# First batch of a fused attention and SiLU kernel: three score buffers instead of two, scores of four heads at once, two value passes in one PSUM bank, and half of w_in loaded in two quarters

## The chip, the cores and the metric

The kernel runs on one core of a Trainium2 chip. The metric is the device time of one execution in microseconds (us); the time before is a median of 391.56 us over three runs (391.54 to 392.47).

## The reference

Attention over 8 batches of 12 heads, 448 tokens and head size 64, and then a feed-forward layer with SiLU over the 3584 tokens:

```
scores = (q @ k^T) / sqrt(64)            # 8 x 12 x 448 x 448
attn   = exp(scores - max) / (sum + 1e-9)
x      = (attn @ v), heads side by side  # 3584 x 768
h      = x @ w_in                        # 3584 x 2048
out    = (h * sigmoid(h)) @ w_out        # 3584 x 768
```

All inputs and the output are float32; the kernel casts to f16 in its loads.

## The kernel before, in words

**Units.** The 12 heads are three groups of four. A unit is one batch and one head group. Batch 0 is cut in two pieces of 224 queries, so it has six units (0 to 5: units 0, 1, 2 are the first piece of the three groups, units 3, 4, 5 the second); `NB0` is 6. Every later batch has three units of 448 queries. A unit of batch 0 has two bursts of scores, the first over 256 keys, the second over 192.

**Attention of one unit.** TensorE writes the scores of a burst (line 346): each of the four heads of the group has its own 32 rows of the array, since head size 64 is split into two passes of 32. The destination is a pair of score tiles `s`, tile y for heads 2y and 2y+1, each of two PSUM banks (`score_banks`, line 336; two buffers, tag "s"). ScalarE turns each tile into `E` by one Exp of 896 elements a row (line 383). TensorE then makes three passes over `E` with four column strips of 32 (line 409): part 0 with a matrix of ones (the sums), parts 1 and 2 with the even and odd columns of `V`. Each part has a PSUM bank of its own (tag "m", four buffers). VectorE turns the sums (450), takes reciprocals (458), turns them back (464) and scales parts 1 and 2 into `xT` (480, one instruction each).

**Feed-forward.** `ffn1` (line 492 inside `times`) multiplies `xT` by `w_in`: for a piece of batch 0, 16 blocks of six matmuls of 224 columns, two blocks to a bank `h`. ScalarE takes the tanh (526), VectorE the gate (561). Then products with `w_out`: `o` for the first two row tiles (`plain`, in pieces of four blocks over 16; blocks 8 to 11 need the third quarter of `w_out`, 12 to 15 the fourth), `p` for the others.

**PSUM.** Eight banks: two `s` tiles of two banks and four `m` banks, for the whole run.

**Loads.** All loads go through GpSimd's DMA queue in one written order: k and q of the three groups of batch 0, V of batch 0 (four loads), q of units 3 and 4, the first half of `w_in` (three loads of 512 KB), q of unit 5, k and q of unit 6, the second half of `w_in`, k and q of unit 7, two quarters of `w_out`, k and q of unit 8, V of batch 1 (twelve loads), the other two quarters of `w_out`, and then batch by batch. Eight semaphores are used in turn, so a load is issued only when the one eight places before it has landed.

**Who sets the order.** A planner written in Python (`Order`, line 82, and the loop from line 1500 on) runs once while the program is built. It gives each operation a cost and a due time, keeps rings of buffers, and writes out the order of each engine's instructions; the engines then run these orders with semaphores. At line 1317 `split` makes the units below `HALVES` (5) issue the scores of heads 0, 1 and of heads 2, 3 as two separate operations; units from 5 on issue all four heads in one, tile y = 0 and y = 1 alternating inside. Matmuls on a tile of zeros (`run_zeros`, line 1491) fill waits of TensorE until the first `ffn1`.

Of the kernel before, what the change touches and what calls it, by code (L numbers as in the profile page):

```python
# [19 lines left out]
DMA_ROW = 0.022  # L20
DMA_RATE = 13570.0
DMA_START = 1.2
DMA_TAIL = 1.0
# [33 lines left out]

def when(deps):

    at = 0.0  # L60
    for d in deps:
        d, slack = d if isinstance(d, tuple) else (d, 0.0)
        if d is None or d.done is None:
            return None
        at = max(at, d.done - slack)
    return at
# [15 lines left out]
class Order:  # L82


    def __init__(self, shy):
        self.now, self.shy = 0.0, shy
        self.free = {"PE": 1.0, "ACT": 2.1, "DVE": 1.2, "POOL": 1.2}
        self.wait = {"ACT": [], "DVE": []}
        self.pool = []
        self.dma_free = 0.0  # L90
        self.out = []
        self.mode = None
        self.busy = {e: 0.0 for e in self.free}
# [8 lines left out]
    def start(self, op):  # L102
        self.emit(op.emit)
        self.free[op.eng] = self.now + op.busy
        self.busy[op.eng] += op.busy
        op.done = self.now + op.busy + op.tail
        if op.then:
            op.then(op.done)
# [12 lines left out]
    def step(self):  # L121
# [26 lines left out]
        elif self.pool:  # L148
            op, took, ring, gate = self.pool[0]
            at = 0.0  # L150
            if ring is not None:
                at = ring.when(1)
            if at is not None and gate is not None:
                g = gate()
                at = None if g is None else max(at, g)
            if at is not None and at <= self.now:
                self.pool.pop(0)
                if ring is not None:
                    ring.take()
                self.start(op)  # L160
                self.dma_free = max(self.dma_free, self.now + DMA_START) + took
                op.done = self.dma_free + DMA_TAIL
                soon.append(self.free["POOL"])
            elif at is not None:
                soon.append(at)
# [4 lines left out]
def kernel(  # L170
# [33 lines left out]
    HALVES = 5  # L204
    NEAR, LATE = 0.15, -2.0
# [14 lines left out]
    ps = ctx.enter_context(tc.tile_pool(name="ps", bufs=1, space=bass.MemoryType.PSUM))  # L220
    ctx.enter_context(
# [114 lines left out]
    def score_banks(n, w, ys):  # L336
        for y in ys:
            pS_t[(n, w, y)] = ps.tile(
                [128, 2, 512], FP32, name=f"s_{n}_{w}_{y}", tag="s", bufs=2
            )  # L340

# [75 lines left out]
    def attend_sums(ns):  # L417
        a = ps.tile([128, 512], FP32, name=f"a_{ns[0]}_0", tag="m", bufs=4)
# [14 lines left out]
    def attend(ns, part, n):  # L433
# [3 lines left out]
        acc[(n, part)] = ps.tile([128, 512], FP32, name=f"a_{n}_{part}", tag="m", bufs=4)  # L437
# [37 lines left out]
    def norm(n, part):  # L475
        b, hg, g0, g1 = units[n]
        nq = 32 * (g1 - g0)
        cc = 2 * hg + part - 1
# [24 lines left out]
    def ffn1(b, f, t0, t1, strips):  # L503
        i = f % blocks(b)
        if i == 0:
            h_t[(b, f, t0)] = ps.tile(
                [128, 512], FP32, name=f"h_{b}_{f}_{t0}", tag="m", bufs=4
            )
# [135 lines left out]
    def pair_product(f, m, strips):  # L644
        if m in (2, 5):
            t = ps.tile([128, 512], FP32, name=f"f_{f}_{m}", tag="m", bufs=4)
# [71 lines left out]
    def product(qd, m, strips):  # L718
        w = {1: rows(2 * qd, 0), 2: rows(2 * qd, 1), 4: rows(2 * qd + 1, 1), 7: rows(2 * qd + 1, 0)}
        w = w[m] if m in w else S_t[(qd, m)]  # L720
        if BANK[m] == m:
            pr_t[(qd, m)] = ps.tile([128, 512], FP32, name=f"p_{qd}_{m}", tag="m", bufs=4)
# [11 lines left out]
    def plain(t, j, f0, f1, strips):  # L734
        if f0 == 0:
            pr_t[("o", t, j)] = ps.tile([128, 512], FP32, name=f"o_{t}_{j}", tag="m", bufs=4)
# [27 lines left out]
    def store(qd, i, j):  # L764
        u, t = divmod(2 * qd + i, NT)
        w, turn = 0, 0
        while w < 4:
# [3 lines left out]
            if b == B - 1:  # L771
                n = 2
# [29 lines left out]
    s_ring, m_ring, e_ring = Ring(2), Ring(4), Ring(NE)  # L802
# [43 lines left out]
    plan_w_in(0, DFF // 2)  # L846
# [55 lines left out]

    moe = []
# [9 lines left out]
    def queue_ffn1(b, g0, g1):  # L913
        t0, t1, parts = 32 * g0, 32 * g1, []
        for f in range(NFF) if b == 0 else [x for f in range(HF) for x in (f, f + HF)]:

            def run(f=f):
                strips = b > 0 and od.mode == "cols" and bool(qk_seq or av_seq)
                op = Op("PE", NDC * mm(t1 - t0), lambda: ffn1(b, f, t0, t1, strips), tail=PE_OUT)
                if warm["on"]:  # L920
                    warm["on"] = False
                    m_ring.give(od.now)
                n = blocks(b)
                if f % n == 0:
                    m_ring.take()
                od.on_pe(op, "cols" if strips else "full")
                ffn1_left[b] -= 1
                if f % n < n - 1:
# [12 lines left out]
                    then=m_ring.give,  # L941
# [81 lines left out]
    def queue_pair_f(f):  # L1023
# [18 lines left out]
        def queue(m):  # L1042
# [6 lines left out]
            def run():  # L1049
                strips = od.mode == "cols" and bool(av_seq)  # L1050
                op = Op("PE", 3 * mm(S), lambda: pair_product(f, m, strips), tail=PE_OUT)
                if m in (2, 5):
                    m_ring.take()
# [10 lines left out]
                elif m == 2:  # L1064
                    read("11", "DVE", lambda: pair_add(f, "p", "B"), [op, done["p"]], m_ring.give)
# [4 lines left out]
                elif m == 3:  # L1070
                    read("12", "DVE", lambda: pair_add(f, "u", "C"), [op, done["u"]], m_ring.give)
# [26 lines left out]
    def sums_w(ms):  # L1098

        for m in ms:  # L1100
# [4 lines left out]
                        0.9,  # L1105
# [10 lines left out]
    def queue_plain(t, j):  # L1116
        parts = []

        def then(at):
            m_ring.give(at)  # L1120
            ost_ring.give(at + STORE)

        def queue(f0, f1):
            def run():
# [4 lines left out]
                if f0 == 0:  # L1129
                    m_ring.take()  # L1130
# [39 lines left out]
    def plan_sums():  # L1170
# [13 lines left out]
        while todo and (todo[0] == 7 or sg_ring.can(1, od.now)):  # L1184
# [4 lines left out]
            for f0 in (0, 4):  # L1189
                deps = [x for f in range(f0, f0 + 4) for x in gates[f] + gates[f + HF]]  # L1190
                if m != 5:
# [5 lines left out]
                            0.34,  # L1197
# [10 lines left out]
    def queue_quad(qd):  # L1208
# [4 lines left out]
        def read(m, deps):  # L1213
            def then(at):
                if m in (2, 3, 4):
                    m_ring.give(at)
# [8 lines left out]
        def queue(m):  # L1225
            first = {6: (1,), 2: (1,), 7: (6, 5), 3: (5, 6) if qd == LAST else (5, 6, 7), 4: (7,)}.get(m, ())

            def run():
                strips = od.mode == "cols" and bool(qk_seq or av_seq)
                op = Op("PE", HF * mm(OH), lambda: product(qd, m, strips), tail=PE_OUT)  # L1230
                if BANK[m] == m:
                    m_ring.take()
# [82 lines left out]
    for ns in jobs:  # L1315
# [7 lines left out]
        av_seq += [(ns, 0, ns[0])] + [(ns, part, n) for n in ns for part in (1, 2)]  # L1323
    pace = {"next": 0.0}

# [17 lines left out]
    def run_qk():  # L1343
# [22 lines left out]
        for y in ys:  # L1366
# [6 lines left out]
                    tail=0.2,  # L1373
                    then=s_ring.give,
# [48 lines left out]
    def run_av():  # L1423
# [4 lines left out]
        m_ring.take()  # L1428
        op = Op(
            "PE",  # L1430
            (3 if two and part == 0 else 4) * mm(nq) + 0.013,
# [3 lines left out]
        if part == 2:  # L1435
# [16 lines left out]
    def after_sums(ns, op, nq):  # L1452
        wide = nq / 960.0 + 0.15
        turn = od.add(
            Op("DVE", wide, lambda: inverse(ns, 0), [op] + inv_op[-1:], -10, then=m_ring.give)
# [16 lines left out]
    def after_av(n, part, op, nq):  # L1472
# [3 lines left out]
            nq / 960.0 + 0.13,  # L1476
# [3 lines left out]
            then=m_ring.give,  # L1480
        )
        x_op[(b, 2 * hg + part - 1, g0)] = od.add(x)
# [3 lines left out]
        if part == 2:  # L1486
# [4 lines left out]
    def run_zeros(n):  # L1491
        if "z" not in warm:
            warm["z"] = ps.tile([128, 512], FP32, name="z", tag="m", bufs=4)
        for _ in range(n):
            nc.tensor.matmul(  # L1495
                out=warm["z"][:, 0:128], lhsT=zeros, rhs=zeros, start=True, stop=True
            )

    m_ring.take()
    while True:  # L1500
# [44 lines left out]
        if warm["on"] and od.free["PE"] <= od.now and wait > 0.06 and od.now > 0.9:  # L1545
# [4 lines left out]
            od.on_pe(Op("PE", n * each, lambda n=n: run_zeros(n)), "full")  # L1550
# [35 lines left out]
```

## Time and profile before

| what | value |
|---|---|
| time, median of three runs | 391.56 us |
| the profiled execution: time | 391.46 us |
| the profiled execution: span | 389.7 us |
| TensorE busy (zeros included) | 382.6 us |
| ScalarE busy | 251.9 us |
| VectorE busy | 273.7 us |
| GpSimd busy | 89.1 us |
| DMA queue of the loads | 24784 packets, 22.82 MB |

The span is what the profiler sees between the first and the last instruction; the time has 1.76 us around it. An engine's busy time is the union of its instructions. In the timeline, consecutive instructions of one line are merged into one row with their count, and a row's end overlaps the next row's start by the pipeline's length, so the distance between starts tells what a group costs. "Landing" of a load is counted from the start of its issue on GpSimd.

### The profile page before, as it was taken

The numbers are of one execution on the slowest core, as the hardware profiler recorded it, in microseconds if no ns is written. First come the engines' busy times: TensorE is split into PE (matmuls) and PEld (weight loads), VectorE is DVE, ScalarE is ACT, GpSimd is POOL, SyncE is SP. The second block draws the span as 40 slices with busy tenths as digits, with TensorE's granted clock in tenths as the row PEclk, the third lists the DMA queues.
The fourth block names the chain that finished last, engine by engine and source line by source line (L and its number), as shares of the span: only waits on it lengthen the run. The fifth ranks groups of instructions, "written<-read, shape, count | busy, mean of one in ns | idle before, by whom it ended". The sixth has DMA issues, their size and how long they took to land.

```text
span 389.7 us, 10594 instructions
## 1 busy us (share of the span) xinstructions
PE 382.6 (98%) x4357; PEld 205.2 (53%) x4357; DVE 273.7 (70%) x554; ACT 251.9 (65%) x383; POOL 89.1 (23%) x173
## 2 busy tenths in 40 slices
PE   8999999999999999999999999999999999999995
PEld 6668765444545444554444454544445655556663
DVE  2466575999988597976969778567869984547441
ACT  4977876797674878757796665466783248882220
POOL 7632455515005152700524133000000000000000
PEclk9999999999999999999999999999999999999999
DMA  7999999928226663854456556202000130001333
GB/s 114 204 210 210 164 155 171 212 36 119 45 56 105 129 98 47 115 109 83 65 85 97 82 97 116 38 0 62 24 0 3 43 96 25 2 0 43 91 97 98
DMA packets 35361, 34.52 MB, mean 89 GB/s; under 512 B 11376, under 2 KB 33776, under 8 KB 35312
## 3 DMA queue, kind: packets, MB, share of 16 engines
q0 software_dynamic: 24784, 22.82, 40.1%
q1 hardware_dynamic: 9952, 10.33, 9.9%
q8 instruction: 34, 0.56, 0.6%
q10 hardware_dynamic: 576, 0.69, 0.6%
q14 instruction: 15, 0.12, 0.1%
HBM read 45.61 MB, written 11.01 MB: 145 GB/s over the span
## 4 chain that ended last, share of the span: by engine, by line
PE 97%; DMA 1%; issue 0%; ACT 0%; POOL 0%; DVE 0%; POOLq 0%
PE p L492 31%; PE h L492 29%; PE s L346 13%; PE a L409 11%; PE f L492 8%; PE o L492 3%; PE a L425 2%; DMA rq<-in_q_dram 1%; PE z L1495 1%; ACT E L383 0%; POOL rk L255 0%; ACT ost L785 0%; DVE rq L333 0%; POOLq L1570 0%
## 5 line engine op out<-in xcount | busy, mean ns | idle before, releaser
L383 ACT ACTIVATE E<-s 128x896 f16<-128x896 f32 (+1 forms) x172 | 149.0, 914 | 44.1 <-PE s L346 43.1
L492 PE MATMUL h<-xT,w_in_t 128*32 128x448 f16 (+2 forms) x1086 | 117.0, 336 | 0.0
L492 PEld LDWEIGHTS <-w_in_t 128*128 128x128 f16 (+1 forms) x1158 | 71.2, 97 | 56.1 <-issue 10.9
L526 ACT ACTIVATE th<-h 128x448 f16<-128x448 f32 x96 | 52.4, 546 | 33.5 <-PE h L492 27.8
L492 PEld LDWEIGHTS <-G 128*128 128x128 f16 (+1 forms) x568 | 43.0, 98 | 32.7 <-issue 5.0
L785 ACT COPY ost<-p 128x384 f32<-128x384 f32 x52 | 25.0, 480 | 51.3 <-PE p L492 44.9
L570 DVE SCALAR_TENSOR_TENSOR G<-th,h 128x448 f16<-128x448 f16 (+1 forms) x80 | 44.3, 560 | 18.3 <-ACT th L526 16.8
L280 POOL DMA_DIRECT2D V<-in_v_dram x88 | 48.3, 560 | 13.6 <-DMA w_out_t<-in_moe_w_out_dram 6.1
L346 PE MATMUL s<-rq,KT 32*128 32x448 f16 (+4 forms) x768 | 49.4, 337 | 0.9 <-DVE rq L333 0.5
L492 PE MATMUL p<-w_out_t,G 128*128 128x384 f16 (+1 forms) x376 | 49.2, 326 | 0.0
L409 PE MATMUL a<-E,V 128*32 128x448 f16 (+2 forms) x864 | 42.3, 333 | 0.9 <-issue 0.9
L492 PEld LDWEIGHTS <-S 128*128 128x128 f16 (+1 forms) x456 | 30.2, 97 | 22.3 <-issue 1.5
L261 POOL DMA_DIRECT2D rq<-in_q_dram x27 | 15.1, 559 | 100.8 <-PE s L346 73.2
L492 PE MATMUL p<-D,S 128*128 128x384 f16 (+1 forms) x280 | 36.7, 326 | 0.0
L480 DVE SCALAR_TENSOR_TENSOR xT<-a,rdn 128x448 f16<-128x448 f32 (+1 forms) x54 | 30.5, 570 | 7.9 <-PE a L409 5.2
L346 PEld LDWEIGHTS <-KT 32*128 32x128 f16 (+2 forms) x864 | 16.7, 98 | 28.7 <-issue 26.5
L791 DVE TENSOR_TENSOR ost<-p,ost 128x384 f32<-128x384 f32 x39 | 21.5, 552 | 14.6 <-PE p L492 11.5
L409 PEld LDWEIGHTS <-V 128*32 128x32 f16 (+1 forms) x864 | 20.4, 96 | 19.9 <-issue 7.9
L394 DVE TENSOR_TENSOR T<-E,E 128x1792 f16<-128x1792 f16 x20 | 21.7, 1085 | 8.4 <-ACT E L383 8.4
L394 DVE TENSOR_TENSOR T<-T,E 128x1792 f16<-128x1792 f16 x20 | 21.6, 1081 | 7.7 <-ACT E L383 7.7
L315 DVE STREAM_TRANSPOSE KT<-rk 128x256 f32<-128x256 f32 (+3 forms) x48 | 16.6, 384 | 6.4 <-DMA rk<-in_k_dram 5.8
L492 PE MATMUL p<-D,G 128*128 128x384 f16 (+1 forms) x128 | 19.1, 326 | 0.0
(68 smaller groups left out, 329.7 us busy)
## 6 DMA issues: line engine op xcount, KB each, us to landing
out_dram<-ost SPq DMA_DIRECT2D x194, 48.0 KB, 1.6
rk<-in_k_dram POOLq DMA_DIRECT2D x24, 224.0 KB, 5.3
rq<-in_q_dram POOLq DMA_DIRECT2D x21, 224.0 KB, 5.3
w_in_t<-in_moe_w_in_dram POOLq DMA_DIRECT2D x6, 512.0 KB, 11.3
w_out_t<-in_moe_w_out_dram POOLq DMA_DIRECT2D x4, 768.0 KB, 14.0
V<-in_v_dram POOLq DMA_DIRECT2D x43, 64.0 KB, 4.1
V<-in_v_dram POOLq DMA_DIRECT2D x40, 48.0 KB, 3.8
out_dram<-ost SPq DMA_DIRECT2D x8, 96.0 KB, 2.1
```

The costliest lines, as they stand in the source:

```text
L280: nc.gpsimd.dma_start(out=VT[b][32 * x : 32 * (x + 1), hs, 0:count, :], in_=v[b, hs].rearrange("h (i g) d -> i h g d", g=TPP)[:, :, first ...
L315: nc.vector.transpose(out=pairs[:, x:y, 0:count], in_=t[:, first : first + count * (y - x)].rearrange("p (x c) i -> p x c i", c=count),)
L346: nc.tensor.matmul(out=pS[p0 : p0 + 32 * (x1 - x0), h % 2, at : at + nq], lhsT=KT[(b, hg)][32 * h : 32 * (h + 1), c, x0:x1, :, e], rhs=QT[ ...
L383: nc.scalar.activation(out=E[(n, w)][0:kr, 2 * y : 2 * y + 2, 0:nk], in_=pS_t[(n, w, y)][0:kr, :, 0:nk], func=AF.Exp, scale=attn_scale,)
L394: nc.vector.tensor_tensor(out=T[n], in0=T[n] if step else E[(n, 0)], in1=E[(n, step + 1)], op=ALU.add,)
L409: nc.tensor.matmul(out=a[32 * h : 32 * (h + 1), 0:nq], lhsT=w, rhs=e[k0:k1, h, at : at + nq], start=start, stop=stop,)
L480: nc.vector.scalar_tensor_tensor(out=x3(b, cc)[:, cc % 3, 32 * g0 : 32 * g1], in0=acc[(n, part)][:, 0:nq], scalar=0.5, in1=rdn_t[n].rearra ...
L492: nc.tensor.matmul(out=out[i : i + cut], lhsT=w[:, i : i + cut], rhs=x, start=start, stop=stop, skip_group_check=True,)
L526: nc.scalar.activation(out=th, in_=h_t[(b, f, t0)][:, 0:n], func=AF.Tanh)
L570: nc.vector.scalar_tensor_tensor(out=dst[:, f, at + lo : at + hi], in0=th_t[(b, f, t0)][:, lo - t0 : hi - t0], scalar=1.0, in1=h_t[(b, f, ...
L785: nc.scalar.copy(out=ost(qd, *OUT[m]), in_=bank(qd, BANK[m]))
L791: nc.vector.tensor_tensor(out=t, in0=bank(qd, BANK[m]), in1=t, op=ALU.add)
```

## The change

Five things, all for batch 0, and new figures in the planner.

1. A third `s` buffer for batch 0: every third tile comes from a pool `early` (two banks). While it is open there are two `m` banks instead of four. After the last Exp of unit 5 it is closed and a pool `late` gives banks 2 and 3 back (`hand_over`, `open_banks`). The four-bank ring becomes `Banks`, which names each bank.
2. `HALVES` goes from 5 to 0: all units of batch 0 issue the scores of four heads in one operation.
3. In batch 0, parts 1 and 2 become part 3: 32 matmuls into one bank, columns 0 to 223 and 256 to 479, and one VectorE instruction of 2 x 224 scales both (two instructions for units 1 and 4, whose two parts lie in different `xT` tiles).
4. The first half of `w_in` is loaded as two quarters: six loads of 128x2x512 in place of three of 128x2x1024. The three loads of the first quarter stand first.
5. The zeros go to whichever bank is free.

The planner gets an overlap of consecutive instructions (0.09 us on ScalarE, 0.07 us on VectorE), an earlier release of a score tile after its Exp (0.06 us instead of 0.2), other DMA figures with a window of eight loads, and `LATE` -0.5 instead of -2.0 (how soon after V's landing a value pass may be placed). Stores of the last batch's rows go out in wider pieces (one of 128 rows where the tile allows it), except in the last pair of row tiles.

```diff
-DMA_ROW = 0.022
+OVERLAP = {"ACT": 0.09, "DVE": 0.07}
+LOADS, DMA_SLOW = 8, 1.1
+DMA_ROW = 0.006
...
-DMA_TAIL = 1.0
+DMA_TAIL = 1.5
...
-        self.free[op.eng] = self.now + op.busy
+        self.free[op.eng] = self.now + op.busy - OVERLAP.get(op.eng, 0.0)
...
-    HALVES = 5
-    NEAR, LATE = 0.15, -2.0
+    HALVES = 0
+    NEAR, LATE = 0.15, -0.5
...
         for y in ys:
-            pS_t[(n, w, y)] = ps.tile(
-                [128, 2, 512], FP32, name=f"s_{n}_{w}_{y}", tag="s", bufs=2
-            )
+            third = n < NB0 and len(pS_t) % 3 == 2
+            pS_t[(n, w, y)] = (early[0] if third else ps).tile(
+                [128, 2, 512], FP32, name=f"s_{n}_{w}_{y}", tag="s", bufs=1 if third else 2
+            )
...
+    def open_banks():
+        early[1].close()
+        late.append(ctx.enter_context(tc.tile_pool(name="late", bufs=1, space=bass.MemoryType.PSUM)))
...
-        acc[(n, part)] = ps.tile([128, 512], FP32, name=f"a_{n}_{part}", tag="m", bufs=4)
+        if part < 3:
+            acc[(n, part)] = psum_bank(f"a_{n}_{part}")
+        else:
+            acc[(n, 3)] = acc[(n, 1)] = psum_bank(f"a_{n}_3")
+            acc[(n, 2)] = acc[(n, 1)][:, 256:512]
+            attend_part(ns, 1, n)
+            attend_part(ns, 2, n)
+            return
+        attend_part(ns, part, n)
...
+        if part == 3:
+            both = acc[(n, 3)].rearrange("p (k q) -> p k q", k=2)[:, :, 0:nq]
+            x0 = 2 * hg
+            for x, y in ((x0, x0 + 1), (x0 + 1, x0 + 2)) if x0 % 3 == 2 else ((x0, x0 + 2),):
+                rdn = rdn_t[n].rearrange("p (k g) i -> p k (g i)", k=1)
+                nc.vector.scalar_tensor_tensor(
+                    out=x3(b, x)[:, x % 3 : x % 3 + y - x, 32 * g0 : 32 * g1],
+                    in0=both[:, x - x0 : y - x0],
+                    scalar=0.5,
+                    in1=rdn.to_broadcast([128, y - x, nq]),
+                    op0=ALU.mult,
+                    op1=ALU.mult,
+                )
+            return
...
-                n = 2
+                n = 4 if w == 0 and qd < LAST else 2
...
-    s_ring, m_ring, e_ring = Ring(2), Ring(4), Ring(NE)
+    s_ring, m_ring, e_ring = Ring(3), Banks((0, 1)), Ring(NE)
...
-    plan_w_in(0, DFF // 2)
+    plan_w_in(0, DFF // 4)
+    plan_w_in(DFF // 4, DFF // 2)
...
-        av_seq += [(ns, 0, ns[0])] + [(ns, part, n) for n in ns for part in (1, 2)]
+        av_seq.append((ns, 0, ns[0]))
+        av_seq += [(ns, part, n) for n in ns for part in ((3,) if ns[0] < NB0 else (1, 2))]
...
-                    tail=0.2,
-                    then=s_ring.give,
+                    tail=0.06,
+                    then=hand_over if (n, c, y) == (NB0 - 1, 1, 1) else s_ring.give,
```

## The prediction

> **What bounds the kernel now.** I read the page's span, busy times and slices first, then TensorE's waits, then the timelines. One execution spans 389.7 us and took 391.46, 0.10 under the median of 391.56; I add the difference in span to the median.
>
> ```profile
> span 389.7 us, 10594 instructions
> ...
> PE 382.6 (98%) x4357; PEld 205.2 (53%) x4357; DVE 273.7 (70%) x554; ACT 251.9 (65%) x383; POOL 89.1 (23%) x173
> ...
> PE   8999999999999999999999999999999999999995
> ...
> GB/s 114 204 210 210 164 155 171 212 36 119 45 56 105 129 98 47 115 109 83 65 85 97 82 97 116 38 0 62 24 0 3 43 96 25 2 0 43 91 97 98
> ```
>
> TensorE is busy 98% of the span. The slices are 9.7 us long: only the first is not full, and there the loads already move over 200 GB/s, until about 39 us. TensorE's waits:
>
> ```profile
> PE z L1495 <- DVE zeros L228: 1.0, 1, 1.0
> PE a L409 <- issue: 0.9, 1, 0.9
> PE s L346 <- DVE rq L333: 0.5, 1, 0.5
> PE s L346 <- ACT E L383: 0.4, 1, 0.4
> ```
>
> They sum to 2.8 us, all before 28 us, but zeros count as busy. So time can only come from the start: zeros, waits, and work that TensorE does badly. Its timeline there:
>
> ```profile
> 6.03 0.60 PE L346 MATMUL s<-rq,KT 32*128 32x224 f16 x16 [0.48 <-DVE rq L333]
> ...
> 16.54 0.57 PE L346 MATMUL s<-rq,KT 32*128 32x224 f16 x8
> 17.04 0.57 PE L409 MATMUL a<-E,V 128*32 128x224 f16 x16
> 17.54 0.57 PE L346 MATMUL s<-rq,KT 32*128 32x224 f16 x8
> ...
> 25.44 0.58 PE L346 MATMUL s<-rq,KT 32*128 32x224 f16 x16
> ...
> 27.84 0.86 PE L409 MATMUL a<-E,V 128*32 128x224 f16 x27 [0.86 <-issue]
> ...
> 33.73 0.95 PE L409 MATMUL a<-E,V 128*32 128x224 f16 x32
> 34.61 1.32 PE L492 MATMUL h<-xT,w_in_t 128*128 128x224 f16 x12
> ```
>
> From 16 to 24 us a half (8 matmuls, two heads) costs 0.50 us and a pass 0.50 us, so TensorE gives ScalarE one tile per 1.00 us; an Exp takes 0.91 us, and five in a row took 4.17 us, one per 0.81. TensorE is the bound there. From 10 to 16 us zeros stand between the halves: ScalarE and the landing of V bound that part.
>
> **Four heads at once.** At 25.44 sixteen matmuls of four heads cost 0.51 us, as much as one half. But the two halves at 6.03, back to back, also cost 0.54: halves overlap already where nothing lies between them. Of the 20 halves of units 0 to 4, the 18 others cost 0.50 each; nine bursts at 0.51 replace them: 4.4 us less work, of which the part that zeros surrounded gives nothing.
>
> **Third buffer, shared bank.** A burst now needs two of three tiles free, so it starts when the last Exp but one ends and must finish within the last one: 0.06 us to see the release (7.55 to 7.61), 0.60 for the burst, 0.07 to ScalarE, against 0.71 from that end to the next due start. It just fits, so I let Exps run at 0.81 until unit 5. TensorE needs 0.51 x 2 + 1.27 = 2.3 us a unit (three passes together took 1.27 at 24.24), ScalarE 3.3. The spare holds zeros and 12 matmuls of ffn1, which the issue order puts behind unit 4's bursts. They need the first quarter of w_in by about 20 us; three half-size loads behind q of unit 4 (landed 9.3 + 5.9 = 15.2) at 1.25 us each give 19.0. Two banks make a chain per unit: pass 0.50, turn 0.42, double pass 0.88, scaling about 0.6, and hops, 2.7 us, under ScalarE's 3.3.
>
> **What comes late next: q of unit 5.** It landed at 13.1 + 10.2 = 23.3. In VectorE's new order its turn (0.41) stands ahead of unit 3's scaling, which frees a bank, and in TensorE's order unit 5's first burst stands ahead of unit 4's passes. The last Exp of unit 4 ends near 23.8, so all wait for this load: 23.6 (below) + 0.41 + hops = 24.1 against 25.44. From there burst 0.51; scaling of unit 3 until 24.75; pass until 25.25; the gate of the first h, then the double pass 25.35 to 26.2; second burst to 26.75; 24 matmuls of ffn1 2.4; a burst 0.51; unit 5's passes 1.27; about 31.0. Before, the same work ended at 34.61. TensorE's lead is 3.6 us.
>
> **w_in in quarters.** 768 packets of 2 KB become 1536 of 1 KB. The loads are a single stream at about 205 GB/s from 15 to 45 us, so what it costs delays every later load.
>
> ```profile
> L289 POOL DMA_DIRECT2D w_in_t<-in_moe_w_in_dram x2: 696/706/715, 10.7 to 11.5; - x2
> ...
> DMA to landing us min/median/max: 9.4/10.3/11.2
> ```
>
> The three loads landed at 17.7, 20.1 and 22.7: 2.5 us for 256 packets, 9.8 ns each. V's loads of 384 packets of 512 B landed 1.05 us apart, 2.7 ns each. A line through both gives 0.4 ns a packet; times 768 is 0.3 us. Lower bound 0, V's rate for all gives 0.9, and the page's mean over the queue (0.401 x 16 x 389.7 us / 24784 = 101 ns of one engine, against 156) gives 9.7 us instead of 7.5, so 2.2. I take 0.3. [...] GpSimd's three more issues of 0.70 us fall where it waits up to 2.2 us between issues.
>
> **The end of the lead: w_out.** The third and fourth quarters are issued behind V of batch 1:
>
> ```profile
> L297 POOL DMA_DIRECT2D w_out_t<-in_moe_w_out_dram x2: 757/761/765, 48.9 to 49.7; - x2
> ...
> DMA to landing us min/median/max: 8.0/10.0/12.1
> ```
>
> ```profile
> 64.24 0.61 PE L346 MATMUL s<-rq,KT 32*64 32x448 f16 x16
> 64.78 2.77 PE L492 MATMUL o<-w_out_t,G 128*128 128x384 f16 x16
> ```
>
> They land at 56.9 and 61.8, now 57.2 and 62.1. The matmuls at 64.78 are the first that need the fourth. The new order asks for it eight o matmuls (1.30 us) earlier in the work: 31.0 + (64.78 - 34.61) - 1.30 = 59.9. For the third it asks 3.7 us before that, 56.2. TensorE stands about 1.0 us at the third and 1.2 at the fourth, and goes on at 62.15. Against 64.78 that is 2.63 less; the 1.30 of o comes after; so 1.3, and 0.1 for one switch fewer: **1.4 us less**. Behind that point both orders hold the same matmuls (133 and 132 changes between full array, row strips and column strips, about 0.1 us each), and from h of the last batches on the same sequence. Merged stores are hidden: the last pair keeps its pieces. The sum is 391.56 - 1.4 = 390.1.
>
> **Rivals.**
> - *The lead survives.* If w_out lands by 59.9 (its gap from the third to the fourth quarter, 4.9 us, was 3.7 for the first two: 39.6, 43.3) all 3.6 us stay, less 0.2 for small waits: 388.1. Against it: V's twelve small loads stand before it, paced by GpSimd.
> - *Dear packets.* With 2.2 us the fourth quarter lands at 64.0: 1.9 above my case, 392.0. For it: only the page's mean, which holds V's small packets.
> - *No lead.* If the two-bank chain or the late q costs 3 us more in batch 0, TensorE reaches w_out after it has landed; with no lead left 391.5.
> - *Waits at every burst, the slower case.* The planner now releases a tile 0.14 us earlier after an Exp and lets two Exps overlap by 0.09 each; TensorE's order is fixed, so a burst placed too early stops it with all ffn1 behind it. In the trace the burst at 35.87 starts 0.64 us after its Exps end (33.50 + 1.73 = 35.23), the one at 38.78 0.57 later; 0.32 of that goes, and 0.25 stays, which speaks against. There are 74 bursts after batch 0: at 0.05 us each 3.7 us, net 2.3, 393.9. It decides from 0.02 us a burst, where the gain is gone.
>
> One clock question: the wait of 0.86 at 27 us was followed by matmuls at 0.10 us as before, clock 1.00. [...] No wait in this trace is long enough to show it; I give that 0.03.
>
> **How the numbers follow.** Forecast 0.50 (two thirds of it beyond 0.3%, since 1.4 stands close to 1.17), lead survives 0.14, dear packets 0.11 (mostly within), no lead 0.08, waits at every burst 0.14, clock 0.03. A measurement of this kernel can tell about 0.3% (1.17 us). Faster 0.33 + 0.14 + 0.01 = 0.48; slower 0.14 + 0.04 = 0.18; within 0.34. The range, 388.0 to 392.0, runs from the surviving lead to dear packets and leaves out about 0.18.
>
> **What would show it.** Exps at 0.81 apart up to 22 us; TensorE waiting for q of unit 5 near 24; unit 5's passes over by 31.0; waits of TensorE on w_out's DMA of about 2.2 us between 56 and 62.2; no waits after. A fourth quarter landing away from 62.1, or any row of waits of s on E above 1 us, makes it wrong.

## The result and the profile after

The changed kernel takes 390.32 us (median of nine runs, 389.23 to 392.86) against 391.57 us in the same number of runs of the kernel before: a ratio of 0.9969, 95% interval 0.9955 to 0.9982. One run of before, at 401.89 us, was in a slower state and is left out of the ratio. The forecast was 390.1 us. The profiled execution took 390.32 us, its span is 388.5 us (before 389.7). The lines of its page, in the order of those shown of before:

```profile
span 388.5 us, 10985 instructions
...
PE 380.1 (98%) x4546; PEld 204.6 (53%) x4546; DVE 270.2 (70%) x550; ACT 250.4 (64%) x383; POOL 91.2 (23%) x176
...
PE   7989999999999999999999999999999999999995
...
PEclk9989999999999999999999999999999999999999
...
GB/s 111 200 208 211 168 151 205 208 18 78 78 86 79 136 95 47 127 101 90 104 79 100 42 63 171 13 2 62 23 3 2 41 88 35 0 2 41 84 102 102
...
q8 instruction: 35, 0.57, 0.6%
```

TensorE's busy time fell by 2.5 us and the span by 1.2. The third slice (19.4 to 29.1 us) is new: TensorE is no longer full there, and its granted clock is below full. Its waits:

```profile
PE a L457 <- issue: 1.7, 1, 1.7
PE s L394 <- DVE rq L365: 1.1, 2, 0.7
PE z L1580 <- DVE zeros L260: 1.0, 1, 1.0
PE z L457 <- issue: 0.4, 1, 0.4
PE a L457 <- DVE xT L541: 0.2, 1, 0.2
```

The columns are the total, the count and the longest, in us. "issue" means that nothing in the profile released the instruction. (The 0.4 us at z is the first value pass; it goes on at 14.98, when the last load of V has just landed, at 14.9.) There is no line for `w_out`, where the prediction had 2.2 us, and none for scores waiting on an Exp. TensorE's timeline in the first batch, and where `o` asks for the last quarter of `w_out`:

```profile
18.66 0.37 PE L457 MATMUL a<-E,V 128*32 128x224 f16 x7
20.74 1.22 PE L457 MATMUL a<-E,V 128*32 128x224 f16 x25 [1.71 <-issue]
...
22.11 0.94 PE L394 MATMUL s<-rq,KT 32*128 32x224 f16 x16
22.98 1.30 PE L564 MATMUL z<-xT,w_in_t 128*128 128x224 f16 x6
...
25.34 0.75 PE L564 MATMUL z<-xT,w_in_t 128*128 128x224 f16 x6
...
26.91 0.58 PE L394 MATMUL s<-rq,KT 32*128 32x224 f16 x16
...
32.97 0.95 PE L457 MATMUL a<-E,V 128*32 128x224 f16 x32
33.85 1.32 PE L564 MATMUL h<-xT,w_in_t 128*128 128x224 f16 x12
...
62.06 2.12 PE L564 MATMUL o<-w_out_t,G 128*128 128x384 f16 x12
```

Seven of the 32 matmuls of unit 2's value pass run, then TensorE stands for 1.71 us in the middle of the pass: same line, same operands, same bank. Then matmuls are slow: six of ffn1 take 1.30 us at 22.98, and 0.75 at 25.34. Unit 5's passes are over at 33.85 (next row's start), not at 31.0; before it was 34.61. The lead is 0.76 us, not 3.6. TensorE's slices of 1 us (busy and count, granted clock, DMA share, GB/s) show the slow stretch:

```profile
20.00:21.00 1.00, 0.26 (x12) 1.00 1.27 209
21.00:22.00 1.00, 1.00 (x25) 0.52 1.22 200
22.00:23.00 1.00, 1.00 (x18) 0.50 1.24 212
23.00:24.00 1.00, 1.00 (x10) 0.50 1.18 212
24.00:25.00 1.00, 1.00 (x26) 0.77 1.13 213
```

The clock is halved from 21.0 to 24.5 us, for 3.4 us, from 0.3 us behind the wait on.

### The profile page after: what moved, and what is told of

Its sections match the earlier page's. It is cut to its first block, busy times and chain, and to the rows that moved or that the text cites. A ratio compares the mean times of both kernels' runs of the same rounds, so it can differ in the third digit from the quotient of the medians.

```text
span 388.5 us, 10985 instructions
## 1 busy us (share of the span) xinstructions
PE 380.1 (98%) x4546; PEld 204.6 (53%) x4546; DVE 270.2 (70%) x550; ACT 250.4 (64%) x383; POOL 91.2 (23%) x176
## 4 chain that ended last, share of the span: by engine, by line
PE 96%; DMA 1%; issue 1%; DVE 0%; POOL 0%; ACT 0%; POOLq 0%
PE p L564 31%; PE h L564 29%; PE s L394 11%; PE a L457 11%; PE f L564 8%; PE o L564 3%; PE a L473 2%; DMA rk<-in_k_dram 1%; PE z L1580 1%; PE z L564 0%; PE z L457 0%; DVE KT L347 0%; POOL rk L287 0%; DVE xT L541 0%; POOL rq L293 0%
## 5 line engine op out<-in xcount | busy, mean ns | idle before, releaser
L564 PE MATMUL h<-xT,w_in_t 128*32 128x448 f16 (+2 forms) x1308 | 115.8, 340 | 0.0
L564 PEld LDWEIGHTS <-w_in_t 128*32 128x32 f16 (+1 forms) x1392 | 72.0, 97 | 56.3 <-issue 11.6
L855 ACT COPY ost<-p 128x384 f32<-128x384 f32 x52 | 25.0, 480 | 51.5 <-PE p L564 48.6
L564 PE MATMUL p<-w_out_t,G 128*128 128x384 f16 (+1 forms) x352 | 49.2, 326 | 0.0
L394 PE MATMUL s<-rq,KT 32*128 32x448 f16 (+4 forms) x768 | 45.3, 340 | 1.2 <-DVE rq L365 1.1
L457 PE MATMUL a<-E,V 128*32 128x448 f16 (+3 forms) x832 | 40.8, 338 | 1.7 <-issue 1.7
L293 POOL DMA_DIRECT2D rq<-in_q_dram x27 | 14.9, 553 | 98.1 <-PE s L394 84.3
L457 PEld LDWEIGHTS <-V 128*32 128x32 f16 (+1 forms) x864 | 21.2, 97 | 20.1 <-issue 6.8
L394 PEld LDWEIGHTS <-KT 32*128 32x128 f16 (+2 forms) x864 | 14.1, 99 | 28.1 <-issue 25.0
L552 DVE SCALAR_TENSOR_TENSOR xT<-a,rdn 128x448 f16<-128x448 f32 x42 | 25.1, 615 | 1.2 <-PE a L457 0.2
L564 PE MATMUL p<-w_out_t,S 128*128 128x384 f16 (+1 forms) x128 | 19.1, 327 | 0.0
```

Of the source, the lines that this page charges most:

```text
L394: nc.tensor.matmul(out=pS[p0 : p0 + 32 * (x1 - x0), h % 2, at : at + nq], lhsT=KT[(b, hg)][32 * h : 32 * (h + 1), c, x0:x1, :, e], rhs=QT[ ...
L457: nc.tensor.matmul(out=a[32 * h : 32 * (h + 1), 0:nq], lhsT=w, rhs=e[k0:k1, h, at : at + nq], start=start, stop=stop,)
L552: nc.vector.scalar_tensor_tensor(out=x3(b, cc)[:, cc % 3, 32 * g0 : 32 * g1], in0=acc[(n, part)][:, 0:nq], scalar=0.5, in1=rdn_t[n].rearra ...
L564: nc.tensor.matmul(out=out[i : i + cut], lhsT=w[:, i : i + cut], rhs=x, start=start, stop=stop, skip_group_check=True,)
L855: nc.scalar.copy(out=ost(qd, *OUT[m]), in_=bank(qd, BANK[m]))
```

## What holds TensorE in the middle of a pass: the theory

The wait of 0.86 us that the prediction quoted from before also stood in the middle of a pass. Count TensorE's instructions in program order (a matmul is two, its weight load and itself): before goes on with its 477th matmul, instruction 954, the changed kernel with its 349th, instruction 698, and 954 - 698 = 256. The page's "instruction" queue moved 34 packets for 8714 instructions of TensorE before and 35 for 9092 after, each 0.57 MB / 35 = 16 KB: one for each 256.

**Theory F (fetch).** TensorE's instructions come in pieces of 256 over the DMA engines that the loads also use (the page of the changed kernel counts both queues on the same 16 engines: 0.6% of their span for the 35 packets, 40.0% for the loads). The borders are at instructions 186 + 256 k (to within an instruction or two, as counted in the trace). While the loads fill the engines, a piece is there between 5 and 6 us after TensorE passed the border before (5.62 and 5.64 us in the two waits of the table); where 256 instructions take less, TensorE stands. The trace's instruction packets, against the borders (us):

```
kernel   border passed   next packet starts   ends    next border: goes on at   wait
before   698 at 22.22    25.51                26.40   954 at 27.84              0.86
after    442 at 15.10    18.49                19.47   698 at 20.74              1.71
after    698 at 20.74    24.40                25.36   954 at 27.13              none
before   1466 at 44.97   45.59                46.54   1722                      none
```

In these two kernels a packet starts 2.9 to 3.7 us after the border under full loads (until about 39 us) and 0.5 to 2.2 us after the next three borders, where the loads thin out.

**Rivals.** *S*: a semaphore that the profile does not show, of the two-bank chain for instance; the wait then stays with the value pass of unit 2. *Q*: the six quarter loads of `w_in`. *P*: for the gain, the parts of the change themselves, whatever the borders do.

## The experiments

Unless told otherwise, each is the changed kernel with one edit.

**Four zero matmuls in one.** The same columns, 51 matmuls instead of 102, so that every border falls 102 instructions further on in the work.

```diff
+        wide = zeros.rearrange("p (o f) -> p o f", o=1).to_broadcast([128, 4, 128])
+        for _ in range(n // 4):
+            nc.tensor.matmul(out=spare[i].rearrange("p (k f) -> p k f", k=4), lhsT=zeros, rhs=wide, start=True, stop=True)
-        for _ in range(n):
+        for _ in range(n % 4):
```

> The changed kernel, with each four zero matmuls of 128 columns put into one of 512: the same TensorE time, 102 zero instructions become 51, everything behind them stands 102 rows earlier in TensorE's instruction list (two rows a matmul). Theory F: the wait of 1.71 us inside unit 2's value pass is TensorE's instruction fetch. Instructions come in pieces of 256 rows; a piece is asked for when the piece before it begins, and arrives 5.6 us later while the loads fill the DMA engines (27.84 - 22.22 before, 20.74 - 15.10 after). Then no wait stands in unit 2's value pass; it stands at the new border, unit 3's sums (row 698), ends 5.6 us after unit 3's first burst passed row 442 (near 16.5, so near 22.1), and is 1.0 to 1.6 us long. Theory S: the pass waits for a semaphore that the profile misses (V's load, or VectorE freeing the bank); then it stays in unit 2's value pass at 1.7 us. F: time 389.0 to 390.0, since unit 5 waits for its q load anyway; S: 390.3.

389.29 us (388.98 to 390.21), ratio 0.994 [0.9925, 0.9955]. Its timeline:

```profile
21.44 0.55 PE L457 MATMUL a<-E,ones 128*32 128x224 f16 x13 [0.66 <-issue]
...
27.45 0.28 PE L457 MATMUL a<-E,V 96*32 96x224 f16 x3 [0.69 <-issue]
```

Unit 2's value pass runs whole. The wait stands at 698 again, which is now in unit 3's sums, and ends 5.55 us after 442 was passed; it is shorter than the 1.0 to 1.6 us expected. With two short waits the clock stays whole. S falls: the wait stays with the count of instructions, not with the pass or its bank. Q is tested by itself below.

**More zeros.** 28 of the first 47 cut in two of 64 columns: 56 instructions more, borders earlier in the work.

```diff
-        for _ in range(n):
+        for k in range(n):
+            for lo in (0, 64) if n == FIRST and k < 28 else (None,):
```

> The changed kernel, with 28 of the first 47 zero matmuls cut into two of 64 columns: the same TensorE time, 56 rows more ahead of everything. Theory F: the border moves back to unit 2's sums (row 698); row 442 falls into the zeros ahead of unit 2's second burst, near 13.2, so the wait ends near 18.9 and is about 1.2 us long; the next border falls into unit 3's value pass. Theory S: the wait stays in unit 2's value pass, 1.7 us. F: time 389.5 to 390.3; S: 390.3.

389.58 us (388.21 to 393.46), ratio 0.9952 [0.9926, 0.9978]. The wait moved the other way, into unit 2's sums, and the kernel with more zeros cannot be told from the one with fewer: what changed in both is where the borders lie.

```profile
18.61 0.35 PE L457 MATMUL a<-E,ones 96*32 96x224 f16 x5 [1.09 <-issue]
...
24.53 0.66 PE L457 MATMUL a<-E,V 96*32 96x224 f16 x18 [0.57 <-issue]
```

**Loads held back.** A copy on GpSimd that reads the first `xT` ahead of the loads of `w_in` leaves the DMA engines nearly empty from 14 to 18 us (a share of 0.07 to 0.10).

```diff
+    def hold_loads():
+        t = const.tile([128, 1], FP16, name="held")
+        nc.gpsimd.tensor_copy(out=t, in_=x3(0, 0)[:, 0, 0:1])
...
+    od.load(1, 4, hold_loads, gate=lambda: when([x_op.get((0, 0, 0))]))
```

> The changed kernel, with a small GpSimd copy ahead of w_in's first load that reads the first scaled value pass, so that no load is issued between q of unit 4 and about 16.5 us. The borders fall on the same instructions as in the changed kernel (rows 442 and 698 in the value passes of units 0 and 2). Theory F: the DMA engines run empty near 15.5, just after row 442 passes at 15.1, the fetch comes sooner, and the wait in unit 2's value pass falls below 0.6 us. Theory S (bank or V): it stays 1.7 us. Every later load is 2 to 2.5 us later, so w_in and q of unit 5 come late: time 391.0 to 393.0 by either.

394.19 us (393.55 to 394.76), ratio 1.006 [1.0045, 1.0075]: the late loads cost more than the expected 391.0 to 393.0. What it tells apart is at 18 us, in TensorE's slices and its timeline:

```profile
14.00:16.00 2.00, 2.00 (x76) 1.00 0.07 13
16.00:18.00 2.00, 2.00 (x77) 1.00 0.10 9
```

```profile
18.05 0.96 PE L457 MATMUL a<-E,V 128*32 128x224 f16 x32
```

The order up to here is that of the changed kernel and so is border 698, inside this pass. The pass runs without a wait, 3.6 us after border 442; in the changed kernel TensorE went on 5.64 us after it, and its packet started only 3.39 us after it. So with the engines at a share of 0.07 to 0.10 the piece was there at least 2 us sooner. With loads back (from 19 us), the next border waits 1.25 us.

**First half of w_in in one load each, as before.**

```diff
-    plan_w_in(0, DFF // 4)
-    plan_w_in(DFF // 4, DFF // 2)
+    plan_w_in(0, DFF // 2)
```

> The changed kernel, with the first half of w_in loaded as before (three loads of 512 KB). The borders fall on the same instructions as in the changed kernel. Theory F: the wait in unit 2's value pass stays at 1.5 to 1.9 us, since the load queue is just as full; the first ffn1 matmuls come at 22 to 23 us anyway, when all of the half has landed (22.7 before), so the quarters bought nothing: time 390.0 to 390.8. The rival here: the quarters are what lets ffn1 start early, and without them TensorE stands up to 2 us more: 391.5 to 392.5.

391.37 us (390.73 to 392.77), ratio 0.9995 [0.9983, 1.0006].

```profile
20.59 0.86 PE L457 MATMUL a<-E,V 128*32 128x224 f16 x26 [1.81 <-issue]
...
25.70 1.31 PE L564 MATMUL z<-xT,w_in_t 128*128 128x224 f16 x12
```

The wait and the halved clock stay, so the quarters do not cause them, and Q falls. But nearly the whole gain is gone: without the early quarter the first 12 matmuls of ffn1 stand at 25.70, not at 22.98 and 25.34. The expected 390.0 to 390.8 were missed; the rival range, 391.5 to 392.5, is the nearer one.

**The other parts undone one at a time, and the kernel before with wide zeros.**

First the scores in two halves, then the value passes in banks of their own, then two score buffers with four banks:

```diff
-    HALVES = 0
+    HALVES = 5
...
-        av_seq += [(ns, part, n) for n in ns for part in ((3,) if ns[0] < NB0 else (1, 2))]
+        av_seq += [(ns, part, n) for n in ns for part in (1, 2)]
...
-            third = n < NB0 and len(pS_t) % 3 == 2
+            third = False
-    s_ring, m_ring, e_ring = Ring(3), Banks((0, 1)), Ring(NE)
+    s_ring, m_ring, e_ring = Ring(2), Banks((0, 1, 2, 3)), Ring(NE)
```

> The first batch's scores in two halves of 8 matmuls on two strips again, three score buffers, two single banks and everything else as changed. The prediction's step 1 says that four strips take 4.4 us of work off the first batch by part counts, and that only the Exps' pace (0.81 us) kept that from the end. If that step mattered for the end: 391.0 to 391.6 us, with waits of the Exps on scores. If the end is set by instruction fetch (fewer zeros here, 69 for 102, so the border after row 698 falls into unit 2's sums and the one after row 954 into ffn1, whose 0.11 us matmuls take 24 rows in 1.3 us and leave the fetch time): a wait without a releaser ahead of row 699 that ends 5.5 us after row 442, none at row 955, and 389.8 to 390.6 us.

> Value passes of the first batch one by one again, each in a bank of its own and with its own normalisation, the rest as changed. With two single banks until unit 5's last Exp, the bank of a pass is free only when VectorE has read it, so each pass waits for a read if banks are the limit: waits of TensorE on VectorE at the passes of units 0 to 4, and 391.0 to 392.0 us. If fetch sets the pace, the borders lie where they lie in the changed kernel (rows 186 and 442 are the same instructions), the wait comes at row 699 (a burst of unit 4 instead of unit 2's value pass) and is again 1.2 to 1.8 us long, and the time is 390.0 to 390.8 us.

> The kernel before, with nothing but each four zeros of 128 columns made one of 512: the same TensorE time, 66 rows fewer, no part of the change. By fetch: the border at row 442 moves from a burst of unit 3 into unit 1's sums (18.2 us), row 698 to the end of unit 2's last pass (23.6 us in the timeline of before, 5.4 us later), row 954 into unit 5's burst at 29.3 us (5.7 us later): each piece comes just in time, the wait of 0.86 us in unit 4's value pass goes, any other is under 0.3 us, and the time is 390.6 to 391.2 us. If the wait is no matter of where the borders lie, it stays in unit 4's value pass and the time is 391.5 us.

> Two score buffers and four single banks in the first batch, the rest as changed (four strips, value passes in a shared bank, quarters). With two buffers a burst waits for the Exp of the burst before the last, so the next Exp starts one burst (0.51 us) and two hand-overs later than the one before ended: Exps some 1.1 to 1.3 us apart instead of 0.82, with waits of TensorE on ScalarE or zeros in between (161 of them), unit 5's last Exp at 25 us or later, and 391.0 to 393.0 us if the third buffer is what carries the first batch. By fetch alone, with more zeros between the passes the rows are used up more slowly, the waits without a releaser shrink to under 0.5 us, and the time is 389.5 to 390.5 us in spite of the slower Exps.

Halves: 391.66 us, ratio 0.9997 [0.9982, 1.0013]. Own banks: 392.29 us, 1.0006 [0.9995, 1.0016]. Two buffers: 395.19 us, 1.0077 [1.006, 1.0093]. Each part undone takes back the gain or more: P holds, and the pure fetch times (389.5 to 390.8) are missed by all three. All three are even above the ranges given for the parts (391.0 to 391.6, 391.0 to 392.0, 391.0 to 393.0). TensorE still stands at borders, but in the first at 954, where no wait was expected, and not at 698, where one was (line of the halves, then of own banks):

```profile
27.47 1.21 PE L564 MATMUL h<-xT,w_in_t 128*128 128x224 f16 x11 [0.90 <-issue]
```

```profile
21.38 0.45 PE L394 MATMUL s<-rq,KT 32*128 32x224 f16 x9 [1.61 <-issue]
```

With own banks the wait is inside a burst of unit 4 instead of a value pass, as F has it. With two buffers no such wait exceeds 0.23 us, and it is still the slowest: the bursts stand 2.2 to 2.8 us apart (17.07, 19.30, 22.08, 24.56).

Wide zeros in the kernel before: 391.26 us, ratio 0.9982 [0.9973, 0.9991], against an expected 390.6 to 391.2.

```profile
29.36 0.61 PE L346 MATMUL s<-rq,KT 32*96 32x224 f16 x16 [1.04 <-issue]
```

The wait left unit 4's value pass and stands at border 954, now ahead of unit 5's second burst, about as long as before. The expected "just in time" was wrong: its 29.3 us were read from the timeline of before, which held the old wait of 0.86 us; without that, TensorE stood at the border at 28.3, and the piece came 5.84 us after the border before (23.52). The 0.2% that the fewer zeros and the moved borders gain shows in the ten runs, but not in the profiled one (391.54 us, unit 5's passes over at 34.67).

**Fewer zeros still, w_out earlier, sums ahead.** Three kernels, their edits in this order. The first makes each group of zeros of as few matmuls as can be (41). The second also loads the third and fourth quarter of `w_out` ahead of V of batch 1's groups 1 and 2. The third also orders the sums of the next unit ahead of each value pass.

```diff
+        while n > 0:
+            k = min(n, 4)
+            n -= k
...
+    plan_v(1, 0, 1)
+    plan_w_out(NFF // 2, 3 * NFF // 4)
+    plan_w_out(3 * NFF // 4, NFF)
-    for hg in range(NG):
+    for hg in range(1, NG):
         plan_v(1, hg, hg + 1)
...
+    for i, x in enumerate(values):
+        ahead += sums[i + 1 : i + 2] + [x]
+    av_seq = ahead + av_seq[len(first) :]
```

> The changed kernel with every group of zeros made of as few matmuls as can be (up to four of 128 columns in one of up to 512): 41 zero matmuls instead of 102 (the one-in-four version had 51), the same columns streamed. The borders after rows 442, 698 and 954 come to lie in unit 1's value pass, in unit 3's sums and in unit 5's second burst. By fetch: the piece after row 442 is there 5.6 us after that row, so with row 442 near 16.4 us the wait at row 699 ends at 22.0 us and is at most 0.5 us, the one at row 955 at 27.6 us and at most 0.4 us, the clock stays whole, unit 5's passes are over by 32.2 us and the time is 388.7 to 389.5 us. If the gain of the wide zeros came from something else than the place of the borders, a further 10 fewer matmuls change nothing or move the time at random: up to 390.3 us.

> As with the fewest zeros, and in addition the third and fourth quarter of w_out loaded ahead of V of batch 1 for groups 1 and 2 (two loads moved up by two places on GpSimd's queue). The prediction's step 5 took these two quarters to be what a lead is lost to (landings 57.2 and 62.1 us). If a lead of about 2.3 us at unit 5 already meets them, o's matmuls come earlier and the time falls by another 0.5 to 1.5 us, to 387.5 to 388.6 us. If the lead is still smaller than what the quarters allow (landing 61.4 us, first asked 62 us), nothing is gained: 388.7 to 389.6 us, or some tenths more if V of batch 1 comes too late for unit 7.

> As the kernel before this one in the call, and in addition the sums of the next unit ahead of the value pass of each unit in the first batch, so that VectorE's turn-over of the sums lies under a value pass. Same matmuls, another order. The borders come to lie in unit 2's sums, unit 2's value pass and ffn1. By fetch: waits at row 699 (ends 5.6 us after row 442) up to 1.5 us since the dense stretch lies whole between the two borders, none at row 955, 388.7 to 390.0 us, and a halved clock with 390.0 or more if the wait reaches 1.7 us. If semaphores (the wait for the sums' reciprocal) set the pace instead, the order ahead gains 0.3 to 0.8 us over the other: 388.0 to 388.8 us.

389.63 us (389.3 to 390.25), ratio 0.9942 [0.9927, 0.9956]; 389.23 us (388.92 to 389.48), 0.9929 [0.9914, 0.9944]; 388.61 us (388.37 to 389.18), **0.9919 [0.9902, 0.9935]**, faster than before and than the change. Among the three the intervals overlap, so no step from one to the next is clear of noise. In the first, the waits moved to where F put them, but are longer than expected:

```profile
22.54 0.28 PE L457 MATMUL a<-E,ones 96*32 96x224 f16 x3 [0.73 <-issue]
...
28.45 0.50 PE L394 MATMUL s<-rq,KT 32*96 32x224 f16 x9 [0.99 <-issue]
```

Ten fewer zeros gain nothing over the 51. In the third, one wait of 0.42 us is left, where up to 1.5 us had been expected; the burst behind q of unit 5 stands at 24.57 and unit 5's passes are over at 31.43 (the prediction had 24.1 and 31.0, the latter with 36 matmuls of ffn1 ahead of it; here there are 30, and the other six cost 0.6 us later):

```profile
22.00 0.28 PE L457 MATMUL a<-E,V 96*32 96x224 f16 x4 [0.42 <-issue]
...
24.57 0.58 PE L394 MATMUL s<-rq,KT 32*128 32x224 f16 x16
...
29.77 1.72 PE L457 MATMUL a<-E,V 128*32 128x224 f16 x64
31.43 0.57 PE L394 MATMUL s<-rq,KT 32*128 32x448 f16 x8
```

Its 388.61 us lie just below what fetch gave (388.7 to 390.0) and within the rival's range, in which the sums' turn-over under a value pass is what gains (388.0 to 388.8). Which of the two it is stays open.

**The third without the earlier w_out.**

> The fewest zeros and the sums ahead, as in the fastest kernel so far (388.61 us; unit 5's passes over at 31.49 us, a lead of 3.1 us over before), but with the third and fourth quarter of w_out loaded where the change loads them, behind V of batch 1. The borders in the first batch are the same instructions. Step 5 of the prediction: w_out's last quarters land at about 57.6 and 61.2 us in this place (the changed kernel: 57.8 and 61.4), while TensorE, with a lead of 3 us, asks for them at about 57.5 and 60.1 us: a wait of 0.8 to 1.3 us on the fourth quarter, or ffn1 work put ahead of it and given back later, and 389.2 to 390.0 us. If the lead is free of w_out, the time is that of the fastest kernel, 388.4 to 388.8 us, and its whole gain over the other two comes from the order of the sums.

390.55 us (389.22 to 392.57, twelve runs), ratio 0.9973 [0.9958, 0.9987]. That is above both expected ranges, 1.9 us over the kernel with `w_out` earlier, whose interval lies clear of this one, and also above the fewest zeros without the sums ahead (389.63). So the place of `w_out`'s last quarters is worth about 1.9 us once TensorE comes early. The profiled execution is its fastest, 389.22. There `w_out` is met on the edge: issued at 49.2 and 50.0, landed 7.0 and 10.0 later, at 56.2 and 60.0.

```profile
54.71 2.41 PE L564 MATMUL o<-w_out_t,G 128*128 128x384 f16 x12
...
60.15 2.12 PE L564 MATMUL o<-w_out_t,G 128*128 128x384 f16 x12
```

The first group needs the third quarter from its ninth matmul on and took 0.29 us longer than the 2.12 of an unhindered one; the second needs the fourth quarter 0.15 us after it landed. In the changed kernel the two landed at 57.8 and 61.4. The slower eleven runs have no profile; that `w_out` is late in them is likely with a margin of 0.15 us, but only argued.

## Why the total was right and the lead was not

Two numbers per profiled execution settle where leads go: the end of unit 5's passes, and the matmuls of ffn1 that stand ahead of it, since those not yet done come behind it. One costs 0.10 us (24 from 29.66 to 32.07 in the changed kernel); "at 36" is the end moved to the 36 that before and the change have, and "rest" is the span behind that.

```
kernel                      unit 5 over  ffn1   at 36   span    rest    longest wait without releaser
before                      34.61        36     34.61   389.7   355.1   0.86
after                       33.85        36     33.85   388.5   354.7   1.71, clock halved
before, wide zeros          34.67        36     34.67   389.8   355.1   1.04
four zeros in one           32.39        36     32.39   387.2   354.8   0.69
more zeros                  32.28        36     32.28   388.0   355.7   1.09
loads held back             35.51        48     34.31   391.8   357.5   1.25
w_in in halves              33.10        18     34.90   389.5   354.6   1.81, clock halved
scores in halves            34.82        48     33.62   389.0   355.4   0.90
own banks                   33.85        18     35.65   390.4   354.7   1.61, clock halved
two score buffers           40.13        78     35.93   393.8   357.9   0.23
fewest zeros                33.07        36     33.07   387.7   354.7   0.99
  + w_out earlier           32.98        36     32.98   387.7   354.7   1.21
  + sums ahead              31.43        30     32.03   386.6   354.6   0.42
  sums ahead, w_out late    31.83        30     32.43   387.4   355.0   0.57
```

Counted so, the rest is 354.6 to 355.1 us in ten of the fourteen: what is gained by then reaches the end. In three of the others TensorE waited for `w_out` (0.4 us with loads held back, 0.5 with scores in halves, 1.2 with two score buffers), in the fourth, more zeros, for VectorE near 80 us (0.7).

1. *Four heads at once* held: a burst behind another group costs about 0.5 us (in the fastest kernel the burst at 24.57 is followed by ffn1 at 25.08; in the changed kernel some before 17 us, among zeros, cost 0.6 to 0.9), and halves give back the gain (391.66).
2. *Exps 0.81 apart* held at first: 12 Exps from 6.51 on in 9.89 us, 0.82 each. After that ScalarE waited for scores, 0.47 us at 16.4 and 2.59 us up to 23.08, where TensorE stood: the pace was predicted to 22.
3. *q of unit 5* landed at 24.1 (predicted 23.6), but the burst behind it stood at 26.91, since TensorE was late for another reason. **This is the step that failed**: "unit 5's passes over by 31.0". The missing 2.85 us fit the fetch wait of 1.71 and the halved clock, of which 3.4 us at half speed lose up to 1.7 of work. The kernels that differ in their zeros (51, 130, 41, 41 with `w_out` earlier) kept the clock whole and stood at borders for 1.35, 1.66, 1.72 and 2.33 us together; without these waits their unit 5 would be over at 31.0, 30.6, 31.4 and 30.7, an estimate by subtraction. So the rest of the chain was about right, and what it lacked is a term for the fetch of instructions, although the wait of 0.86 us that it quoted was one.
4. *Quarters*: the half of `w_in` landed at 23.5 against 22.7, 0.8 later, not 0.3. Its gain is larger: the early quarter lets 12 matmuls of ffn1 fill TensorE, which the prediction names but does not price, and with halves 1.05 us of the time are gone (391.37 against 390.32).
5. *The lead lost at w_out* did not come, because the lead was not there. The quarters landed at 57.8 and 61.4 (predicted 57.2 and 62.1), the last ahead of the matmuls at 62.06, and TensorE did not wait; 0.76 us of lead came to 1.2 us of span. With 33.85 in place of 31.0 the step's own sum asks for the fourth quarter at 62.7, behind its landing, and gives no wait either. Where the lead was there, the two kernels with the sums ahead show the loss: 390.55 us with `w_out` late, 388.61 with it earlier.

So 390.1 came out near 390.3 because a lead taken 2.8 us too large was followed by a loss of 2.2 us that did not happen. That the time fell so near the forecast is luck; the mechanism that carried it, a denser first batch worth a few us by part counts, is right, and the fastest kernel (388.6), with a lead of 2.6 us and `w_out` out of its way, stands near the rival that the lead survives (388.1). Two small slips in the working change nothing: the three passes that took 1.27 us start at 24.17, not 24.24, and of the page's slices the last, too, is not full.

Of the rivals, *waits at every burst* did not come: the changed kernel has no row of `s` on `E`. *Dear packets* did not come either: the fourth quarter landed at 61.4, not at 64.0. *No lead* came nearest in the lead, but its cause, the two-bank chain or the late q, is not what took it. *The clock* did, with a chance of 0.03. That chance stood on no run: in the trace of before the longest wait without a releaser is 0.86 us, and the clock stayed at 1.00 behind it. What the runs showed: waits of 1.61 us (own banks), 1.71 (the changed kernel) and 1.81 (`w_in` in halves) were each followed by 3.4 us of half clock, which began 0.8, 0.3 and 1.0 us after the wait; the longest wait without a releaser that was not followed by it is 1.25 us (loads held back, 1.00 in every slice from 12 to 30 us). In the nine runs of the changed kernel, the four with a mean granted clock of 1.000 took 389.23 to 390.31 us, the five with 0.990 to 0.996 took 390.32 to 392.86.

What stays open: the spread of the kernel with late `w_out`; what a wait between 1.25 and 1.61 us does to the clock; why it stayed whole in four of the nine runs of the changed kernel, which have no profile; and how much of each undone part's loss is its own and how much comes from the borders and the replanned order that it moves, since no edit here changes one alone.

## What to carry to other kernels

Where a wait stands in the middle of a row of like instructions with no releaser, count the engine's instructions to the next such wait: a constant distance, 256 here, points to instruction fetch. Changing the number of instructions ahead of the dense stretch moves the border; here fewer (389.29 us) and more (389.58) both helped, as the wait was split in two short ones and the clock stayed whole. When small matmuls are packed closer, check that 256 instructions still take longer than a piece needs under the load traffic of that stretch (5.1 to 6.2 us here, at about 205 GB/s). When a milestone is compared between two orders, count the work that stands ahead of it in each. And before a lead is carried to the end, look which later load it will meet: in the kernels with this order of loads, apart from loads held back, the third quarter of `w_out` was issued at 48.6 to 49.9 us whether unit 5 ended early or late.

## What the runs showed of the hardware

- TensorE's instructions come in pieces of 256 (16 KB). Under loads of about 205 GB/s, where TensorE stood for one it went on 5.1 to 6.2 us after the border before, so more than some 45 instructions a microsecond (an estimate, 256 over the middle of that) were not kept up there. In the kernel before and the changed one the packet starts 2.9 to 3.7 us after that border and takes 0.9 to 1.0; at the two waits TensorE went on 1.3 and 1.4 us after its end. At the next three borders, where the loads thin out, it started 0.5 to 2.2 us after the border, and in the run with the loads held back, with the DMA engines at a share of 0.07 to 0.10, TensorE passed the next border without a wait 3.6 us after the one before.
- The granted clock was halved for 3.4 us after single waits of 1.61, 1.71 and 1.81 us among matmuls of 224 columns, from 0.3 to 1.0 us behind the wait on, and stayed at 1.00 after one of 1.25 us. What lies between no run shows.
